# Two heads of the first batch move from the float32 path to the float16 path in a fused attention and feed-forward kernel

## The chip, the cores and the metric

One core of a Trainium2 chip runs the whole program. The metric is the device time in microseconds, the median over several executions. One execution is also profiled: all rows below are from that one, with times from the start of its span.

## What is computed

Eight batches of eight heads, 576 positions of 64 elements; the result of attention is the input x (4608 tokens of 512) of a gated feed forward with 1536 hidden units.

```
scores = (q @ k.T) / 8                       # (8, 8, 576, 576)
cum    = cumsum(max(s, 0))                   # s: (8, 8, 576)
scores = where(causal, -1e9, scores + min(-(cum[:, None] - cum[None, :]), 0))
attn   = exp(scores - max(scores));  attn = attn / (sum(attn) + 1e-9)
x      = (attn @ v) laid out as (8 * 576, 512)
out    = (sigmoid(x @ w_gate) * (x @ w_val)) @ w_out
```

The inputs are float32 or float64 (the weights are decoded from 64-bit words where they come wide), the output is float32.

## The kernel before

The work is written as a loop over ticks `n`, five for each of the 64 heads (`i, t = divmod(n, 5)`), one for each tile of 128 query rows (the first tile has 64). A scheduler of the language then sets the order of each engine's instructions from the order in the program and from priorities: what is written under `first()` goes ahead of the rest. Tiles come from pools with one to ten buffers; a tile that is written again waits for the readers of the old one.

There are two ways through attention.

* The float32 path, for the first `NN` heads (before: `NN = H = 8`, all of batch 0). `n_load` loads a pair's queries and keys; `n_prep` transposes them on TensorE (`nq_ps`, L558) and copies them from PSUM on ScalarE into `nq` and `nk`; `n_s` makes the scores with one float32 matmul for each piece (L575); `n_max` does bias, row maximum (VectorE, L584) and exponential (ScalarE, L587); `n_turn` transposes the weights on TensorE (`nt_ps`, L596) and copies them (L597); `n_av` multiplies with v in float32 (L605); `n_x` transposes x on TensorE (`nx_ps`, L629) and splits it into two float16 parts (L631, L632).
* The float16 path, for all other heads. Every operand is split into a high and a low float16 part. `qk_square`, `qk_scale` and `split_qk` scale and split queries and keys (L357 to L390); one DMA transpose brings them into `T` (L395) and two DMAs swap the halves of the keys (`swap_k`, L400, L401); `split_v` splits v (L430, L431) and copies a part of it by DMA (L436); `s_part` makes the scores with two matmuls for each piece (L446, L447); `bias_row` (L455), `mask_part` (GpSimd, L461) and `max_part` (L471, L474) are bias, mask, maximum and exponential; `p_part` splits the weights (ScalarE L478, VectorE L483 and L491) and transposes them with two DMA transposes into `pt` (L494); `av_part` multiplies with v, 50 small matmuls a head (L506 to L511); `x_part` divides, `split_x` splits x (L527, L528) and transposes it by DMA (L529).

All DMA transposes, loads and swaps of attention are issued from SP's queue, in order; the weights of the feed forward come from ScalarE's queue.

The feed forward works on 18 groups of 256 tokens and 12 slices of 128 hidden units. A unit `(g, f)` is 24 matmuls of 256 columns into `gv` (L657, 48 narrower ones where a group lies in two batches), a tanh (L662), a gate product into `t2` or, in groups 0 and 1, `t2f` (L664), two float16 parts of the hidden slice (`ffn_mid`, L672, L673), and the output matmuls (`ffn_out`, L687). Group 0 needs x of all four pairs of heads of batch 0. From tick `NE` on the first 24 units are given at 1.5 times two units in a tick; with them come the rest of the 18 weight steps (`weight_step`: decode on ScalarE and VectorE, L272 to L275, split, L287 to L293). After them the rate follows the progress of attention, batch by batch; after the last head the remaining units run alone.

In the loop, `NE` stands in three places: where the units begin, as the lower bound of the ticks in which the scores and products of the float16 path have priority, and as the end of the early weight steps.

Of the kernel before, what the change touches and what calls it, by code (L numbers as in the profile page):

```python
# [23 lines left out]
def tile_attention_then_gated_ffn(  # L24
# [12 lines left out]
    B, H, S, D = q.shape  # L37
# [12 lines left out]

    SETS = (((0, 1, 2), (0, 1, 3), 6), ((3, 4), (0, 4), 9))
    PAD = NTL * P - S
    NN = H
    LAG = 3

    ctx.enter_context(nc.allow_low_precision("operands are split into exact high and low parts"))
# [62 lines left out]
    def first(now=True):  # L119
        return tc.high_priority(1000) if now else ExitStack()  # L120
# [287 lines left out]
    def spread_crow(i):  # L408
        spread = nc.gpsimd.partition_broadcast(crow[i], crow[i][0:1] if i > 0 else rel[0:1])  # L409
        if i > NN:  # L410
            tc.keep_in_program_order(spread)

    def load_v(p):
        b, h0 = divmod(2 * p, H)
        t = wp.tile([P, 5, 2, D + 1], F32, tag="v32", name=f"v32_{p}")
        nc.gpsimd.memset(t[64:, 4], 0.0)
        if 2 * p < NN:
            nc.gpsimd.memset(t[:, :, :, D:], 1.0)
# [19 lines left out]
    def s_part(i, t):  # L438
        w = TILES[t][2]
        c0 = S + t * P - PAD  # L440
        lhs = T[i].rearrange("p a n -> p (a n)")[:, c0 : c0 + P]
        pieces = [(0, w)] if w <= 512 else [(0, w // 2), (w // 2, w)]
        S_ps[i, t] = []
        for a, b_ in pieces:
            ps = score_bank(f"s{i}_{t}_{a}")
            nc.tensor.matmul(ps[:, : b_ - a], lhs, T[i][:, 0, a:b_], start=True, stop=False)  # L446
            nc.tensor.matmul(ps[:, : b_ - a], lhs, T[i][:, 2, a:b_], start=False, stop=True)  # L447
            S_ps[i, t].append((ps, a, b_))

    def bias_row(i):  # L450
        if i < NN:
            rl[i] = crow[i]
            return
        r = wp.tile([P, S], F32, tag="rl", name=f"rl{i}")
        nc.vector.tensor_scalar(r, crow[i], qkc[i // 2][1][:, 0:1], None, ALU.mult)  # L455
        rl[i] = r

    def mask_part(i, t):

        q0, m, w = TILES[t]  # L460
        nc.gpsimd.affine_select(rl[i][:, q0:w], rl[i][:, q0:w], pattern=[[-1, m]], compare_op=ALU.is_ge,  # L461
                                fill=-MASKED if i < NN else MASKED, base=0 if i < NN else m - P,
                                channel_multiplier=1)
# [32 lines left out]
    def av_part(i, h_):  # L496
        p, j = divmod(i, 2)
        if i not in AV:
            AV[i] = pp.tile([P, NTL, D + 1], F32, tag="av", name=f"av{i}", bufs=1)
        pt = PT.pop((i, h_))  # L500
        ts, first_block, n = SETS[h_]
        for t, b0 in reversed(list(zip(ts, first_block))):
            for kb in range(t):
                v_ = v16[p][:, kb, j]
                hi, lo = pt[:, b0 + kb], pt[:, LOW[t] + kb]
                nc.tensor.matmul(AV[i][:, t], hi, v_[:, D : 2 * D + 1], start=kb == 0, stop=False)  # L506
                nc.tensor.matmul(AV[i][:, t, 0:D], hi, v_[:, 0:D], start=False, stop=False)  # L507
                nc.tensor.matmul(AV[i][:, t], lo, v_[:, D : 2 * D + 1], start=False, stop=False)  # L508
            v_ = vx[p][:, t, j]
            nc.tensor.matmul(AV[i][:, t], pt[:, b0 + t], v_[:, D : 2 * D + 1], start=t == 0, stop=False)  # L510
            nc.tensor.matmul(AV[i][:, t, 0:D], pt[:, b0 + t], v_[:, 0:D], start=False, stop=True)  # L511

    def x_part(i):
        p, j = divmod(i, 2)
        a = AV.pop(i)
        d = wp.tile([P, 2, NTL], F32, tag="er", name=f"er{i}")
        nc.vector.tensor_scalar(d[:, 0], a[:, :, D], 1e-9 * PSCALE, None, ALU.add)
        nc.vector.reciprocal(d[:, 1], d[:, 0])
        if j == 0:
            xq[p] = wp.tile([P, NTL, P], F32, tag="xq", name=f"xq{p}", bufs=1)  # L520
        nc.vector.tensor_tensor(xq[p][:, :, 64 * j : 64 * j + 64], a[:, :, 0:D],
                                d[:, 1].rearrange("p (t o) -> p t o", o=1).to_broadcast([P, NTL, D]), ALU.mult)

    def split_x(p):
        x16 = wp.tile([P, 2, NTL * P], F16, tag="x16", name=f"x16_{p}", bufs=1)
        src = xq.pop(p).rearrange("p t n -> p (t n)")
        nc.scalar.activation(x16[:, 0], src, AF.Copy)  # L527
        nc.vector.tensor_tensor(x16[:, 1], src, x16[:, 0], ALU.subtract)  # L528
        nc.sync.dma_start_transpose(x_of(*divmod(p, NPAIR)).rearrange("p l (t n) -> p (l t) n", n=P),  # L529
                                    x16.rearrange("p l n -> p (l n)"))  # L530
# [38 lines left out]
    def n_s(i, t):  # L569
        q0, m, w = TILES[t]  # L570
        p, j = divmod(i, 2)
        nS[i, t] = []
        for a, b_ in [(0, w)] if w <= 512 else [(0, w // 2), (w // 2, w)]:
            ps = score_bank(f"s{i}_{t}_{a}")
            nc.tensor.matmul(ps[:, : b_ - a], qT[i][:, q0 : q0 + P], kT[p][:, a:b_], start=True, stop=True)  # L575
            nS[i, t].append((ps, a, b_))
# [143 lines left out]
    load_v(0)  # L720
    n_prep(0)

    NE, NOFF = 44, 87
    FPT = 1.5
    EARLY = 18
    VSQ = 65
# [3 lines left out]
    for n in range(nticks + 12):  # L730
        if n == NTL * EARLY:
            more_room()
        i, t = divmod(n, NTL)
        if i < NN:
            with first():
                n_s(i, NTL - 1 - t)
                if t == 0:
                    bias_row(i)
        elif n < nticks:
            if t == 0:  # L740
                bias_row(i)
            with first(NE <= n < NOFF):
                s_part(i, NTL - 1 - t)
        if 2 <= n < nticks + 2:
            a, z = divmod(n - 2, NTL)
            if a < NN:
                with first():
# [16 lines left out]
                    n_av(a, t_)  # L764

        if t == 1 and NN <= i - 2 < NH:
            with first(NE <= n < NOFF):
                av_part(i - 2, 1)
                av_part(i - 2, 0)
                x_part(i - 2)  # L770
            if i % 2 == 1:
                split_x((i - 2) // 2)
# [165 lines left out]
```

## Time and profile before

| | |
|---|---|
| three runs | 1151.61, 1154.59, 1155.06 us; median 1154.59 us |
| profiled execution | 1150.75 us, span 1149.0 us |
| mean granted TensorE clock | 0.981 |
| TensorE matmul (PE) busy | 1093.9 us, 95% of the span |
| TensorE weight load (PEld) | 856.3 us, 75% |
| VectorE (DVE) | 774.6 us, 67% |
| ScalarE (ACT) | 748.6 us, 65% |
| GpSimd (POOL) | 261.9 us, 23% |
| DMA packets moved | 157.62 MB, mean 137 GB/s |
| largest groups | L657 613.5 us, L687 314.8 us (both PE) |

Shares over the whole span mix stages. The first 260 us hold all of batch 0, the weights and the first groups; most of the rest is feed forward beside attention, and the last 200 us feed forward alone. A matmul's record includes its way through the array, so that records that follow each other overlap; the price of one in a row is the distance of the starts.

### The profile page before, as it was taken

The numbers are of one execution on the slowest core, as the hardware profiler recorded it, in microseconds if no ns is written. First come the engines' busy times: TensorE is split into PE (matmuls) and PEld (weight loads), VectorE is DVE, ScalarE is ACT, GpSimd is POOL, SyncE is SP. The second block draws the span as 40 slices with busy tenths as digits, with TensorE's granted clock in tenths as the row PEclk, the third lists the DMA queues.
The fourth block names the chain that finished last, engine by engine and source line by source line (L and its number), as shares of the span: only waits on it lengthen the run. The fifth ranks groups of instructions, "written<-read, shape, count | busy, mean of one in ns | idle before, by whom it ended". The sixth has DMA issues, their size and how long they took to land.

```text
span 1149.0 us, 30327 instructions
## 1 busy us (share of the span) xinstructions
PE 1093.9 (95%) x11644; PEld 856.3 (75%) x11644; DVE 774.6 (67%) x2393; ACT 748.6 (65%) x1465; POOL 261.9 (23%) x570
## 2 busy tenths in 40 slices
PE   6787889989999999999999999999999999999997
PEld 4566677758777887788777777778877887787775
DVE  6889899866777777775565677777777775222221
ACT  6989778667677777676665677767776765233222
POOL 5625233222132222121211122212222221000000
PEclk9879899999999999999999999999999999999999
DMA  9776778996989888778646488868887764000000
GB/s 266 214 212 164 178 144 183 185 186 135 165 170 174 165 173 169 141 146 145 137 81 136 89 183 164 162 145 181 145 162 144 142 123 88 13 20 19 1 19 19
DMA packets 445102, 157.62 MB, mean 137 GB/s; under 512 B 403551, under 2 KB 435295, under 8 KB 444958
## 3 DMA queue, kind: packets, MB, share of 16 engines
q1 hardware_dynamic: 418398, 127.12, 57.1%
q10 hardware_dynamic: 23040, 16.78, 4.9%
q0 software_dynamic: 3520, 11.80, 3.0%
q8 instruction: 91, 1.49, 0.6%
q14 instruction: 53, 0.43, 0.1%
HBM read 56.92 MB, written 9.58 MB: 58 GB/s over the span
## 4 chain that ended last, share of the span: by engine, by line
PE 51%; issue 25%; DMA 6%; DVE 5%; ACT 3%; POOL 2%; SPq 1%; POOLq 0%; ACTq 0%; DVEq 0%
PE gv L657 28%; PE o L687 14%; PE s L447 2%; PE s L446 2%; DMA v<-in_v_dram 2%; DMA qk<-in_q_dram 1%; POOL rl L461 1%; PE av L506 1%; PE av L508 1%; DVE e L471 1%; PE av L507 1%; DMA pt<-p 1%; SPq L420 1%; ACT e L474 1%; PE av L510 1%
## 5 line engine op out<-in xcount | busy, mean ns | idle before, releaser
L657 PE MATMUL gv<-x,w 128*128 128x256 f16 (+3 forms) x6912 | 613.5, 246 | 5.4 <-DVE t2f L664 2.9
L657 PEld LDWEIGHTS <-w 128*128 128x128 f16 x6912 | 534.0, 98 | 61.7 <-issue 5.3
L687 PE MATMUL o<-w2all,h 128*128 128x512 f16 x1296 | 314.8, 379 | 0.0
L461 POOL TENSOR_SCALAR_AFFINE_SELECT rl<-rl 128x64 f32<-128x64 f32 (+1 forms) x280 | 111.3, 398 | 519.6 <-DVE em L471 464.3
L474 ACT ACTIVATE e<-e,em 128x576 f32<-128x576 f32 x280 | 154.7, 554 | 92.5 <-DVE em L471 90.5
L687 PEld LDWEIGHTS <-h 128*128 128x128 f16 x1296 | 123.7, 98 | 108.0 <-issue 1.7
L662 ACT ACTIVATE th<-gv,scb 128x256 f32<-128x256 f32 (+3 forms) x288 | 111.2, 411 | 138.4 <-PE gv L657 137.6
L664 DVE SCALAR_TENSOR_TENSOR t<-th,gv 128x256 f32<-128x256 f32 x192 | 80.0, 417 | 132.8 <-ACT th L662 131.6
L471 DVE CUSTOM_DVE_ANT_0 e<-s,rl,qkcf 128x288 f32<-128x288 f32 x280 | 135.6, 485 | 29.9 <-PE s L447 24.5
L672 ACT ACTIVATE h<-t,hsc 128x256 f16<-128x256 f32 x192 | 96.6, 503 | 80.1 <-DVE t L664 80.0
L483 DVE SCALAR_TENSOR_TENSOR p<-e,p 128x384 f16<-128x384 f32 x224 | 101.9, 494 | 40.1 <-ACT p L478 39.3
L673 DVE SCALAR_TENSOR_TENSOR h<-t,hsc,h 128x256 f16<-128x256 f32 x192 | 93.1, 485 | 43.4 <-ACT h L672 43.0
L478 ACT ACTIVATE p<-e 128x1152 f16<-128x1152 f32 x112 | 112.1, 1001 | 3.2 <-DMA pt<-p 0.5
L506 PE MATMUL av<-v,pt 128*128 128x65 f16 x560 | 68.0, 193 | 5.3 <-DMA pt<-p 5.3
L446 PE MATMUL s<-T 128*128 128x288 f16 (+2 forms) x246 | 64.8, 281 | 5.2 <-DMA T<-qk 3.8
L695 POOL DMA_DIRECT2D out_dram<-osb x36 | 20.4, 566 | 212.1 <-ACT osb L694 211.2
L507 PE MATMUL av<-v,pt 128*128 128x64 f16 x560 | 68.0, 192 | 0.0
L508 PE MATMUL av<-v,pt 128*128 128x65 f16 x560 | 68.0, 194 | 0.0
L447 PE MATMUL s<-T 128*128 128x288 f16 (+2 forms) x246 | 61.8, 279 | 1.7 <-DMA T<-T 1.6
L506 PEld LDWEIGHTS <-pt 128*128 128x128 f16 x560 | 52.4, 97 | 11.8 <-DMA pt<-p 6.9
L409 POOL PARTITION_BROADCAST cr<-cr x63 | 58.1, 923 | 4.1 <-DMA cr<-cum_d 4.0
L455 DVE TENSOR_SCALAR rl<-cr,qkcf 128x576 f32<-128x576 f32 x56 | 29.1, 519 | 40.0 <-POOL cr L409 39.8
(155 smaller groups left out, 1440.7 us busy)
## 6 DMA issues: line engine op xcount, KB each, us to landing
out_dram<-osb POOLq DMA_DIRECT2D x36, 256.0 KB, 2.9
v<-v SPq DMA_DIRECT2D x56, 162.5 KB
v<-in_v_dram SPq DMA_DIRECT2D x64, 128.0 KB
T<-T SPq DMA_DIRECT2D x82, 72.0 KB
t2f<-in_v_dram SPq DMA_DIRECT2D x20, 288.0 KB
qk<-in_q_dram SPq DMA_DIRECT2D x17, 288.0 KB
qk<-in_k_dram SPq DMA_DIRECT2D x17, 288.0 KB
w2all<-in_moe_w_gate_dram ACTq DMA_DIRECT2D x7, 512.0 KB
```

What stands on the lines that cost most here:

```text
L446: nc.tensor.matmul(ps[:, : b_ - a], lhs, T[i][:, 0, a:b_], start=True, stop=False)
L461: nc.gpsimd.affine_select(rl[i][:, q0:w], rl[i][:, q0:w], pattern=[[-1, m]], compare_op=ALU.is_ge, fill=-MASKED if i < NN else MASKED, bas ...
L471: nc.vector.tensor_tensor_reduce(e_t[t][:, a:b_], ps[:, : b_ - a], rl[i][:, a:b_], c, init, ALU.add, ALU.min, acc)
L474: nc.scalar.activation(e_t[t][:, :w], e_t[t][:, :w], AF.Exp, bias=init, scale=-1.0)
L478: nc.scalar.activation(p_s[h_][:, 0], e_s[h_], AF.Copy, scale=PSCALE)
L483: nc.vector.scalar_tensor_tensor(flat[:, LOW[t] * P : (LOW[t] + t) * P], e_t[t][:, : t * P], PSCALE, flat[:, kb * P : (kb + t) * P], ALU.m ...
L506: nc.tensor.matmul(AV[i][:, t], hi, v_[:, D : 2 * D + 1], start=kb == 0, stop=False)
L657: nc.tensor.matmul(ps[:, gv, a:e], w1[f][:, cc, gv, wl], x_of(b, cc)[:, xl, c0 + a : c0 + e], start=(c == 0), stop=(c == 3 * NC - 1))
L662: nc.scalar.activation(th[:, a:e], ps[:, 0, a:e], AF.Tanh, scale=scb[b][:, f : f + 1])
L672: nc.scalar.activation(h[:, 0], t2, AF.Copy, scale=hsc[:, f : f + 1])
L673: nc.vector.scalar_tensor_tensor(h[:, 1], t2, hsc[:, f : f + 1], h[:, 0], ALU.mult, ALU.subtract)
L687: nc.tensor.matmul(ps[:m], h[:, hl, tt * P : tt * P + m], w2[f][:, wl], start=(f == 0 and c == 0), stop=(f == NF - 1 and c == 2))
```

## The change

`NN` becomes 6: heads 6 and 7, the last pair of batch 0, take the float16 path, so that their queries, keys, weights and x are transposed by DMA and no longer by TensorE. `NE` becomes 47, so that the units of the feed forward are given from tick 47 on instead of 44. The lower bound `NE` goes from the two priorities of the float16 path's scores and products.

```
-    NN = H
+    NN = 6
...
-    NE, NOFF = 44, 87
+    NE, NOFF = 47, 87
...
         elif n < nticks:
             if t == 0:
                 bias_row(i)
-            with first(NE <= n < NOFF):
+            with first(n < NOFF):
                 s_part(i, NTL - 1 - t)
...
         if t == 1 and NN <= i - 2 < NH:
-            with first(NE <= n < NOFF):
+            with first(n < NOFF):
                 av_part(i - 2, 1)
                 av_part(i - 2, 0)
                 x_part(i - 2)
```

What this does to the order of instructions shows at three places. On every engine the order is the same again from head 20 on.

SP's queue, the loads of the fourth pair (heads 6 and 7) before: queries, keys and v, then the next head's row of `cum`.

```order
L540 DMA nqk_3_742<-in_q_dram 96x6x64 x2
L540 DMA nqk_3_742<-in_k_dram 96x6x64 x2
L420 DMA v32_3_747<-in_v_dram 128x4x64 x2
L421 DMA v32_3_747<-in_v_dram 64x2x64
L406 DMA cr6_858<-cum_d_114 1x576
```

The same place now; `T6` and `T7` are the transposed queries and keys of heads 6 and 7.

```order
L347 DMA qk32_3_727<-in_q_dram 96x12x64
L347 DMA qk32_3_727<-in_k_dram 96x12x64
L420 DMA v32_3_776<-in_v_dram 128x4x64 x2
L421 DMA v32_3_776<-in_v_dram 64x2x64
L395 DMA_TRANSPOSE T6_849<-qk16_6_844 128x12x96
L406 DMA cr6_880<-cum_d_114 1x576
L400 DMA T6_849<-T6_849 64x576
L401 DMA T6_849<-T6_849 64x576
L436 DMA v32_3_776<-v16_3_981 64x1300 x2
L395 DMA_TRANSPOSE T7_992<-qk16_7_987 128x12x96
```

The transposes, swaps and copies of the pair stand behind the loads, among the next rows; its `pt` and `x3` transposes follow later in the same queue.

TensorE, where the first unit (`gv0_0`) first reads `x3`, the x of heads 6 and 7, before: behind the first scores of head 9 and the transposes of x3.

```order
L447 MATMUL s9_3_0_1542<-T9_1253 128x448
L629 MATMUL nx_ps_3_3_1296<-ident_88,nx3_1180 128x128 x2
L657 LDWEIGHTS w1_0_66
L657 MATMUL gv0_0_1349<-x3_133,w1_0_66 128x256
L657 LDWEIGHTS w1_0_66
```

The same place now: behind the products of heads 6 and 7 and most of those of head 8 (`av8`).

```order
L510 MATMUL av8_1970<-v32_4_1163,pt1_8_1309 128x65
L511 LDWEIGHTS pt1_8_1309
L511 MATMUL av8_1970<-v32_4_1163,pt1_8_1309 128x64
L657 LDWEIGHTS w1_0_66
L657 MATMUL gv0_0_1454<-x3_133,w1_0_66 128x256
L657 LDWEIGHTS w1_0_66
```

Before, the unit stood ahead of all of head 8's products; now most of them stand ahead of it.

VectorE, ahead of the first unit's gate product (L664), before: it stands at place 285 of the engine's rows, in the middle of head 9's maxima (`em9_3`).

```order
L632 SCALAR_TENSOR_TENSOR x3_133<-nx_ps_3_3_1296,vsc0_327,x3_133 128x256
L367 TENSOR_SCALAR qk1_5_1336<-qk0_5_1334 128x2
L471 ISA e_1_80,em9_3_0_1669<-s9_3_0_1542,rl9_1405,qkcf4_1094 128x448
L471 ISA em9_3_0_1669 128x1
L125 TENSOR_SCALAR xe_w14_1890<-wtot14_1888 128x1
L664 SCALAR_TENSOR_TENSOR t2f_135<-th0_0_1374,gv0_0_1349 128x256
```

The same place now: it is at 332, behind all of head 9's maxima (`em9_0`), the splits of head 10's queries and keys (L390) and a part of head 9's weights (L483, L491).

```order
L390 SCALAR_TENSOR_TENSOR qk16_10_1360<-qk32_5_1287,qksc5_1338,qk16_10_1360 96x6x64
L483 SCALAR_TENSOR_TENSOR p16_1_82<-e_1_80,p16_1_82 128x384
L483 SCALAR_TENSOR_TENSOR p16_1_82<-e_1_80,p16_1_82 128x512
L491 SCALAR_TENSOR_TENSOR p16_1_82<-e_1_80,p16_1_82 128x2x64
L517 TENSOR_SCALAR er8_2011<-av8_1970 128x5
L471 ISA e_0_79,em9_0_0_1762<-s9_0_0_1639,rl9_1344,qkcf4_1108 128x64
L471 ISA em9_0_0_1762 128x1
L664 SCALAR_TENSOR_TENSOR t2f_135<-th0_0_1479,gv0_0_1454 128x256
```

47 more VectorE instructions stand ahead of it.

More of the change, by code (lines that the diff above doesn't have):

```diff
@@ L52, in tile_attention_then_gated_ffn @@
     PAD = NTL * P - S
-    NN = H
+    NN = 6
     LAG = 3
@@ L721, in tile_attention_then_gated_ffn @@
     n_prep(0)
-    NE, NOFF = 44, 87
+    NE, NOFF = 47, 87
     FPT = 1.5
@@ L741, in tile_attention_then_gated_ffn @@
                 bias_row(i)
-            with first(NE <= n < NOFF):
+            with first(n < NOFF):
                 s_part(i, NTL - 1 - t)
@@ L766, in tile_attention_then_gated_ffn @@
         if t == 1 and NN <= i - 2 < NH:
-            with first(NE <= n < NOFF):
+            with first(n < NOFF):
                 av_part(i - 2, 1)
```

## Prediction

> **What bounds the kernel now.** I read the page's slices first, then the busy time by stretch, then TensorE's waits, then the groups by line. In the slices (40 of 28.7 us; tenths busy) TensorE is at 9 from slice 9 on; ahead of that it is not, and there VectorE and ScalarE stand at 7 to 9.
>
> ```profile
> PE   6787889989999999999999999999999999999997
> DVE  6889899866777777775565677777777775222221
> ACT  6989778667677777676665677767776765233222
> ```
>
> The stretches below are cut at VectorE's milestones: the start of head 5's row maxima (80.7), the first unit's gate product in `t2f` (L664, 135.5), unit 11 of group 0 (176.5), unit 11 of group 1 (240.7), unit 1 of group 2 (266.6). Columns: stretch, its length, busy us of PE, PEld, DVE, ACT, POOL, granted clock, DMA share, GB/s.
>
> ```profile
> 80.70:135.50 54.80, 43.29 (x265) 33.52 (x265) 47.54 (x135) 46.06 (x88) 21.70 (x39) 0.84 0.74 187
> 135.50:176.50 41.00, 34.91 (x392) 29.43 (x392) 38.08 (x112) 32.25 (x55) 12.89 (x21) 1.00 0.77 151
> 176.50:240.70 64.20, 60.09 (x618) 46.22 (x619) 54.70 (x193) 50.00 (x99) 19.43 (x41) 1.00 0.91 183
> 240.70:266.60 25.90, 24.32 (x229) 14.97 (x227) 16.80 (x51) 16.37 (x32) 7.29 (x13) 1.00 0.71 167
> 400.00:1149.00 749.00, 741.83 (x8187) 581.07 (x8184) 448.98 (x1418) 441.23 (x874) 125.23 (x298) 1.00 0.57 114
> ```
>
> From 400 us on TensorE is busy 741.8 of 749.0 us (99%), so this part has a fixed length, and the order there is the same before and after. The change is therefore worth what it does to the moment at which the program enters that part. Ahead of it, VectorE is busy 47.5 of 54.8 us (87%) before the first unit and 38.1 of 41.0 (93%) in group 0; TensorE has the higher share only from 176.5 on. TensorE's waits from 100 to 400 us say the same: few, and for transposes and for VectorE.
>
> ```profile
> PE av L506 <- DMA pt<-p: 5.3, 5, 2.0
> PE gv L657 <- DVE t2f L664: 2.9, 3, 1.7
> ```
>
> **TensorE's share of the change.** Heads 6 and 7 lose float32 scores, transposes and products, and get float16 ones. Starts in order of time give the price of one (start, us, engine, line; a float32 matmul has two records):
>
> ```profile
> 103.72 0.97 PE L575 MATMUL s<-nk,nq 128*128 128x448 f32 x2
> 104.53 1.00 PE L605 MATMUL na_ps<-v,p 128*128 128x65 f32 x8
> 105.36 0.76 PE L575 MATMUL s<-nk,nq 128*128 128x320 f32 x2
> 106.86 0.49 PE L596 MATMUL nt_ps<-ident,e 128*128 128x128 f32 x3
> 107.18 0.78 PE L605 MATMUL na_ps<-v,p 128*128 128x65 f32 x6
> 135.60 0.19 PE L506 MATMUL av<-v,pt 128*128 128x65 f16 x1
> 135.63 0.19 PE L507 MATMUL av<-v,pt 128*128 128x64 f16 x1
> 160.93 0.35 PE L446 MATMUL s<-T 128*128 128x448 f16 x1
> 161.12 0.35 PE L447 MATMUL s<-T 128*128 128x448 f16 x1
> ```
>
> A float32 head: 1600 score columns at 0.81 us per 448 are 2.9 us; 15 products at 0.83/4 = 0.21 are 3.1; 15 transposes at 0.32/3 = 0.11 are 1.6; half of a pair's 17 transposes of queries, keys and x, at the same 0.11, 0.9. Together 8.5. A float16 head: 3200 columns at 0.19 per 448 are 1.4, 50 products at 0.03 are 1.5, together 2.9. So TensorE loses 5.6 us a head, 11 in all. By the order all of this lies ahead of the first unit; from the first unit to group 2 TensorE's work is the same within 1 us. There TensorE waits already, so I cost the 11 us at nothing; they would count in full only if TensorE were what delays the first unit.
>
> **VectorE's share.** In the order 287 VectorE instructions stand ahead of the first L664 before, 334 now. The kinds that differ, with their prices (busy us, mean ns of one):
>
> ```profile
> L471 DVE CUSTOM_DVE_ANT_0 e<-s,rl,qkcf 128x288 f32<-128x288 f32 x280 | 135.6, 485 | 29.9 <-PE s L447 24.5 <-POOL rl L461 3.0 <-DVE p L491 0.2
> L471 DVE DVE_READ_ACCUMULATOR2_ANT em<- 128x1 f32 x336 | 27.3, 81 | 0.0
> L584 DVE CUSTOM_DVE_ANT_0 e<-s,cr 128x288 f32<-128x288 f32 (+4 forms) x40 | 16.7, 423 | 6.5 <-PE s L575 3.5 <-POOL cr L461 2.4
> L483 DVE SCALAR_TENSOR_TENSOR p<-e,p 128x384 f16<-128x384 f32 x224 | 101.9, 494 | 40.1 <-ACT p L478 39.3
> L491 DVE SCALAR_TENSOR_TENSOR p<-e,p 128x128 f16<-128x128 f32 x168 | 40.9, 270 | 0.0
> L455 DVE TENSOR_SCALAR rl<-cr,qkcf 128x576 f32<-128x576 f32 x56 | 29.1, 519 | 40.0 <-POOL cr L409 39.8
> L388 DVE SCALAR_TENSOR_TENSOR qk<-qk,qksc,qk 96x384 f16<-96x384 f32 x22 | 13.5, 615 | 1.5 <-ACT qk L387 1.4
> L431 DVE SCALAR_TENSOR_TENSOR v<-v,vsc,v 128x640 f16<-128x640 f32 x28 | 24.7, 882 | 15.0 <-ACT v L430 14.8
> L528 DVE TENSOR_TENSOR x<-xq,x 128x640 f16<-128x640 f32 x28 | 22.9, 820 | 0.8 <-ACT x L527 0.8
> L293 DVE SCALAR_TENSOR_TENSOR w2all<-wa,wscale,w2all 128x1024 f16<-128x1024 f32 x6 | 7.6, 1274 | 0.6 <-ACT w2all L292 0.5
> L367 DVE TENSOR_SCALAR qk<-qk 128x2 f32<-128x2 int32 x28 | 4.7, 168 | 0.7
> L632 DVE SCALAR_TENSOR_TENSOR x<-nx_ps,vsc,x 128x320 f16<-128x320 f32 (+1 forms) x8 | 4.1, 507 | 0.3 <-ACT x L631 0.3
> ```
>
> Row maxima: 15 pieces of L471 more, with their read-outs, at 0.485 + 0.081 = 8.5 us; 12 of L584 fewer, at 0.423 and the same read-out, -6.0. Low parts of the weights p: 10 of L483 (4.9) and 7 of L491 (1.9). Bias rows: 3 of L455 (1.6). Low parts of queries and keys: 3 of L388 and 3 of L390 at 0.615 (3.7). One split of v (0.9), one of x (0.8), one weight split L293 (1.3) that has moved ahead of the unit, 14 small scale instructions at 0.17 (2.4), two L632 fewer (-1.0). The sum is +19.0 us of records. Records of one engine overlap: in these two the next starts 0.37 us after a start whose record lasts 0.44.
>
> ```profile
> 80.71 0.44 DVE L584 CUSTOM_DVE_ANT_0 e<-s,cr 128x288 f32<-128x288 f32 x1
> 81.08 0.07 DVE L584 DVE_READ_ACCUMULATOR2_ANT em<- 128x1 f32 x1
> ```
>
> At 0.07 for each of the 47, 3.3 us go off: +15.7 us of VectorE ahead of the first unit. (Two heads alone are about 10 of it; the rest is head 9's maxima and splits, which the order now puts ahead of the unit too.)
>
> The stretch before the first unit has 54.8 - 47.5 = 7.3 us of idle VectorE. If the new work filled all of it, the unit would be 15.7 - 7.3 = 8 us later; if the idle share stayed at 87%, 15.7/0.87 = 18 us. I take the next stretch's 93%: (47.5 + 15.7)/0.93 = 68.0 us instead of 54.8, +13 us, since there the same mix of float16 heads and weight splits already runs.
>
> **Behind the first unit.** Up to unit 11 of group 0 the orders put equal VectorE work to within three instructions: 0. Up to group 2 VectorE has about 5 us less to do (this is what came earlier), TensorE the same. TensorE is busy 34.9 + 60.1 + 24.3 = 119.3 of 131.1 us there, so between 0 and some 6 us of its idle time could close; I take 2, because its largest wait, for pt, stays. After that the orders are equal and nothing is given back. Sum: +13 - 2 = +11 us.
>
> **ScalarE, DMA and GpSimd** are costed at nothing. ScalarE changes two conversions of p for five copies out of PSUM in each head, nearly even (2.0 against 2.4 us), and adds splits of q, k, v and x against three copies of q and k and one of x, about 1 us a head; VectorE's 87% against ScalarE's 46.1/54.8 = 84% hides it, barely.
>
> ```profile
> L478 ACT ACTIVATE p<-e 128x1152 f16<-128x1152 f32 x112 | 112.1, 1001 | 3.2 <-DMA pt<-p 0.5
> L597 ACT COPY p<-nt_ps 128x384 f32<-128x384 f32 x40 | 18.2, 474 | 3.9 <-PE nt_ps L596 3.5 <-issue 0.3
> ```
>
> SP's queue gets two T transposes, four swaps, two copies of v, four pt transposes and one x transpose. From 80 to 160 us (queue, packets, MB, share):
>
> ```profile
> q1 hardware_dynamic: 22848, 6.75, 42.0%
> q10 hardware_dynamic: 13486, 7.29, 31.9%
> ```
>
> Four float16 heads' T and pt share the 42% (33.6 us), so two heads add at most some 17 us of 80: 74% becomes up to 95%. Cover enough on average, not where w_out's loads on q10 stand.
>
> **Clock.** TensorE's granted clock is 0.84 from 80.7 to 135.5 and 1.00 behind it; with 11 us less work in a longer stretch it has less to do there. The Trainium skill, TensorE: Matmul & The Clock Gate, Part 1, says that an idle window of about 3.4 us halves the clock until a busy one has passed; the rows agree in direction. By that rule the first unit would start cold and lose up to half of 3.4 us, and the sum would be +13 rather than +11.
>
> **Rivals.** (1) Latency: the four float16 heads 6 to 9 have no feed forward beside them, and each waits in turn for T, swap, pt and x through DMA, on SP's one queue. The chain of work shows what each took:
>
> ```profile
> 110.11 5.50 DMA T<-qk
> 172.83 4.45 DMA pt<-p
> 242.40 4.30 DMA x<-x
> ```
>
> VectorE would then stay at 80% or less: (47.5 + 15.7)/0.80 = 79 us, +24 to the first unit, less 2: about +22. Against it: T6 stands right behind v of pair 3 on SP, long ahead of its use. (2) Absorbed: all 7.3 us of idle close (+8) and the 6 us behind it too: +2, no change to be told. For it: more independent streams in a list order. (3) Faster: TensorE, with float32 work at a half clock, is what holds VectorE at 87%; without it VectorE runs full (+8), and all 11.8 us of TensorE's idle time up to group 2 close: 8 - 12 = -4. It decides if the first unit comes less than about 9 us later. Against it: 16 us of VectorE work must fit in 7 us of holes in any case.
>
> **How the numbers follow.** The profiled run took 1150.75 us with a span of 1149.0; +11 makes 1162. The median of the runs is 1154.59, 3.8 above the profiled one, so I predict 1165. Chances: the forecast (+4 to +18) 0.63; latency (+18 to +28) 0.10; absorbed (within 3.5 us either way, which is 0.3% and about what can be told from no change) 0.14; faster (-4 and below) 0.13. Slower 0.73, same 0.14, faster 0.13. The range 1151 to 1175 leaves out the faster case and the upper part of the latency case, about 2 in 10; the likeliest's own is 1158 to 1173.
>
> **What would show it.** The first L664 at 144 to 153 us instead of 135.5, VectorE over 90% busy from 80 us to there, TensorE's busy time there down by about 10 us and its clock not above 0.84; group 2's unit 1 about 11 us late, and a tail from 400 us on that is as long as before. Wrong: a first L664 within 8 us of before, or a long VectorE wait for pt, T or x (then it was latency).

## The result, and the profile after

The changed kernel takes 1167.8 us (median of four runs, 1166.03 to 1170.93) against 1153.1 us for the kernel before (four runs, 1149.59 to 1155.06): a ratio of 1.0119 with a 95% interval of 1.0093 to 1.0146, slower by 14.7 us. The profiled execution took 1170.93 us with a span of 1169.0, the longest of the four; its span is 20.0 us longer than that of the profile before, so times read from the two profiles overstate the loss by some 5 us.

The page's slices of the kernel after (29.2 us each):

```profile
PE   6787488989999999999999999999999999999997
DVE  6888899874778777775666577777777775222221
PEclk9856599999999999999999999999999999999999
```

The clock's slices before (28.7 us each):

```profile
PEclk9879899999999999999999999999999999999999
```

Counted from 0, TensorE's slice 4 falls from 8 to 4 tenths, and its clock is at 5 and 6 tenths in slices 2 to 4, where it was at 7 to 9. VectorE stays at 8 there. From slice 9 on TensorE is as full as it was.

The stretches are cut at the same milestones as in the prediction: head 5's maxima, the first L664, unit 11 of group 0, unit 11 of group 1, unit 1 of group 2; then the last 749 us, and the way from the first L664 to group 2 in one piece. Columns: length, busy us of PE, PEld, DVE, ACT, POOL, granted clock, DMA share, GB/s.

```profile
81.60:155.50 73.90, 46.96 (x305) 34.14 (x305) 64.16 (x175) 53.40 (x89) 26.57 (x43) 0.60 0.82 184
155.50:198.40 42.90, 38.95 (x420) 33.35 (x420) 39.02 (x115) 31.51 (x58) 13.79 (x25) 0.96 0.81 149
198.40:262.10 63.70, 56.52 (x537) 42.62 (x535) 53.76 (x184) 46.82 (x92) 17.19 (x37) 0.95 0.92 176
262.10:290.00 27.90, 27.90 (x256) 17.05 (x255) 12.91 (x37) 14.88 (x30) 5.05 (x11) 1.00 0.51 121
420.00:1169.00 749.00, 742.37 (x8199) 581.72 (x8196) 448.43 (x1418) 440.84 (x873) 124.89 (x298) 1.00 0.57 114
155.50:290.00 134.50, 123.37 (x1208) 93.02 (x1208) 105.68 (x332) 93.21 (x178) 36.03 (x72) 0.96 0.80 156
```

The same last way, before:

```profile
135.50:266.60 131.10, 119.32 (x1237) 90.62 (x1238) 109.57 (x353) 98.62 (x185) 39.61 (x75) 1.00 0.83 170
```

The last 749 us hold the same matmul time as before (742.4 against 741.8 us), so the whole loss arises ahead of them. The stretch before the first unit grew from 54.8 to 73.9 us, and VectorE's work in it from 47.5 to 64.2 us; its share is 87% both times. The DMA share rose from 0.74 to 0.82 of a longer stretch: 54.8 x 0.74 = 40.6 us of all engines' time became 73.9 x 0.82 = 60.6.

VectorE's timeline gives the first gate product and that of unit 1 of group 2:

```profile
155.55 0.41 DVE L664 SCALAR_TENSOR_TENSOR t2f<-th,gv 128x256 f32<-128x256 f32 x1
290.01 0.41 DVE L664 SCALAR_TENSOR_TENSOR t<-th,gv 128x256 f32<-128x256 f32 x1
```

They come 20.0 and 23.4 us later than before (135.5 and 266.6), and by the end the lag is 20.0 again. The lag grows head by head: from the start of head 5's maxima to that of head 8's it goes from 0.9 to 12.2 us (80.7 to 81.6, 119.9 to 132.1).

Before, TensorE's two largest waits from 80 to 136 us were these (line, what it waited for: us, times, longest); beside them it waited 0.3 us for pt.

```profile
PE na_ps L605 <- ACT p L597: 3.3, 4, 1.7
PE s L446 <- DMA T<-qk: 2.3, 1, 2.3
```

After, from 81 to 156 us:

```profile
PE s L446 <- DVE em L471: 8.4, 7, 2.6
PE s L446 <- DMA T<-qk: 4.7, 1, 4.7
PE av L506 <- DMA pt<-p: 4.1, 3, 2.5
...
PE s L447 <- DMA T<-T: 2.1, 2, 1.2
```

and those of SP's queue from 70 to 156 us:

```profile
SPq L420 <- PE na_ps L605: 10.0, 2, 6.2
SPq L395 <- DVE wa L274: 6.4, 1, 6.4
SPq L395 <- DMA t2f<-in_moe_w_out_dram: 5.1, 1, 5.1
```

TensorE waits for VectorE's maxima, and 10.9 us for transfers of the float16 path (T, pt and the swaps), where it waited 2.6 us before. In SP's queue the profile puts 6.4 and 5.1 us of a T transpose's (L395) waits down to a weight's decode and to a load of w_out. No single wait has the size of the loss. The chain of waits in this part passes through three transfers, the longest of them the load of the next pair's queries:

```profile
121.85 5.27 DMA T<-qk
...
133.19 7.01 DMA qk<-in_q_dram
...
142.22 4.44 DMA pt<-p
```

### The profile page after: what moved, and what is told of

Read it like the earlier page. It is cut to its first block, busy times and chain, and to the rows that moved or that the text cites. A ratio compares the mean times of both kernels' runs of the same rounds, so it can differ in the third digit from the quotient of the medians.

```text
span 1169.0 us, 30321 instructions
## 1 busy us (share of the span) xinstructions
PE 1101.5 (94%) x11617; PEld 858.6 (73%) x11617; DVE 785.6 (67%) x2420; ACT 752.8 (64%) x1461; POOL 264.3 (23%) x569
## 4 chain that ended last, share of the span: by engine, by line
PE 58%; issue 20%; DMA 4%; DVE 3%; ACT 2%; POOL 1%; SPq 1%; POOLq 0%; DVEq 0%; ACTq 0%
PE gv L657 32%; PE o L687 16%; PE s L446 3%; PE s L447 3%; PE av L506 1%; PE av L508 1%; PE av L507 1%; DVE e L471 1%; DMA qk<-in_q_dram 1%; DMA v<-in_v_dram 1%; DMA T<-qk 1%; POOL rl L461 1%; DMA pt<-p 1%; PE av L510 1%; PE av L511 1%
## 5 line engine op out<-in xcount | busy, mean ns | idle before, releaser
L657 PE MATMUL gv<-x,w 128*128 128x256 f16 (+3 forms) x6912 | 620.1, 247 | 3.8 <-DVE t2f L664 3.8
L461 POOL TENSOR_SCALAR_AFFINE_SELECT rl<-rl 128x64 f32<-128x64 f32 (+1 forms) x290 | 119.4, 413 | 523.0 <-DVE em L471 463.8
L474 ACT ACTIVATE e<-e,em 128x576 f32<-128x576 f32 x290 | 159.5, 554 | 86.1 <-DVE em L471 84.2
L664 DVE SCALAR_TENSOR_TENSOR t<-th,gv 128x256 f32<-128x256 f32 x192 | 80.1, 417 | 132.3 <-ACT th L662 131.4
L471 DVE CUSTOM_DVE_ANT_0 e<-s,rl,qkcf 128x288 f32<-128x288 f32 x290 | 140.3, 485 | 27.3 <-PE s L447 17.9
L483 DVE SCALAR_TENSOR_TENSOR p<-e,p 128x384 f16<-128x384 f32 x232 | 106.9, 501 | 47.4 <-ACT p L478 46.5
L478 ACT ACTIVATE p<-e 128x1152 f16<-128x1152 f32 x116 | 116.0, 1000 | 5.9 <-DMA pt<-p 2.8
L446 PE MATMUL s<-T 128*128 128x288 f16 (+4 forms) x258 | 69.7, 285 | 15.1 <-DVE em L471 10.2
L506 PE MATMUL av<-v,pt 128*128 128x65 f16 x580 | 72.7, 196 | 10.0 <-DMA pt<-p 9.8
L507 PE MATMUL av<-v,pt 128*128 128x64 f16 x580 | 72.8, 195 | 0.0
L508 PE MATMUL av<-v,pt 128*128 128x65 f16 x580 | 72.6, 197 | 0.0
L447 PE MATMUL s<-T 128*128 128x288 f16 (+4 forms) x258 | 66.4, 284 | 3.0 <-DMA T<-T 3.0
L506 PEld LDWEIGHTS <-pt 128*128 128x128 f16 x580 | 55.4, 99 | 17.3 <-DMA pt<-p 12.1
L507 PEld LDWEIGHTS <-pt 128*128 128x128 f16 x580 | 55.6, 99 | 4.8
```

Of the source, the lines that this page charges most:

```text
L471: nc.vector.tensor_tensor_reduce(e_t[t][:, a:b_], ps[:, : b_ - a], rl[i][:, a:b_], c, init, ALU.add, ALU.min, acc)
L474: nc.scalar.activation(e_t[t][:, :w], e_t[t][:, :w], AF.Exp, bias=init, scale=-1.0)
L478: nc.scalar.activation(p_s[h_][:, 0], e_s[h_], AF.Copy, scale=PSCALE)
L483: nc.vector.scalar_tensor_tensor(flat[:, LOW[t] * P : (LOW[t] + t) * P], e_t[t][:, : t * P], PSCALE, flat[:, kb * P : (kb + t) * P], ALU.m ...
L657: nc.tensor.matmul(ps[:, gv, a:e], w1[f][:, cc, gv, wl], x_of(b, cc)[:, xl, c0 + a : c0 + e], start=(c == 0), stop=(c == 3 * NC - 1))
```

## Experiments

Every run is timed against the kernel before on the same chip; ratios are run to kernel before, with the 95% interval. The expectations set these theories against each other: VectorE's added work (V), the latency of the pair's transfers in turn (L), TensorE's low clock (C), and in the later runs the DMA load, TensorE's own work, and the order that the scheduler makes anew for each program.

The order of instructions tells one thing without a run. With `NN` = 8, `NE` = 47 alone or the changed priorities alone leave the order of before on every engine as it was. With `NN` = 6 that is not so: with `NE` = 44 kept, 266 VectorE instructions stand ahead of the first L664, fewer than the 287 before; with `NE` = 47 it is 334, and every engine has the order of the change, whether the priorities are changed or not. So the later start of the units belongs to the change as much as the path of the two heads does, and no run times `NN` = 6 with `NE` = 44. The nearest is the run on another pair below, which keeps `NE` = 44.

**VectorE's work alone.** The kernel before, with 26 instructions of 576 columns put into VectorE's stream:

```
+        if 30 <= n < 43:
+            for _ in range(2):
+                tc.keep_in_program_order(nc.vector.scalar_tensor_tensor(
+                    load, load, 1.0, load, ALU.mult, ALU.mult))
```

> The kernel before with 26 VectorE instructions of 576 float32 columns more, two in each of the ticks 30 to 42, that stand in program order and touch nothing that is needed (some 0.6 us each, 15.6 us in all). The float32 path, its transposes on TensorE and the place of the units stay. Theory V (VectorE's work ahead of the first units sets when the program enters the part that TensorE bounds): slower by 10 to 16 us, as the change. Theory L (the DMA latency of T, swap, pt and x in heads 6 and 7 sets it): 0 to 5 us slower, since VectorE had 7.3 us of holes there. Theory C (TensorE's clock at a half): under 4 us slower, since TensorE's work is the same.

1166.07 against 1152.72 us, ratio 1.0106 [1.0077, 1.0135]. The stretch before its first unit:

```profile
78.80:144.80 66.00, 49.99 (x316) 38.28 (x316) 62.91 (x164) 49.14 (x90) 27.76 (x40) 0.77 0.69 156
```

VectorE is 95% busy (62.9 of 66.0 us) and the first unit comes 9.3 us late, unit 1 of group 2 13.3 us late (279.9). The 26 instructions are 0.747 us each in the records, 19.4 us in all; 21 of them, 16.2 us, lie ahead of the first unit, about as much as the change's 16.6. VectorE work of this size, with no transfer and no TensorE work changed, is enough to make a loss of this size. The way there is not the change's, though: unit 11 of group 1 is only 1.7 us late (242.4 against 240.7), and the lag is back at unit 1 of group 2, where the next batch is first needed.

**TensorE given more matmuls.** The changed kernel, with 168 matmuls whose results nobody reads:

```
+        if 33 <= n < 47:
+            warm = pp.tile([P, 2, GT], F32, tag="gv", name=f"warm{n}")
+            for c in range(12):
+                nc.tensor.matmul(warm[:, 0], ...)
```

> The changed kernel with 12 matmuls of 256 columns in each of the ticks 33 to 46, on a weight tile, into PSUM tiles that nobody reads: 168 matmuls, 18 us of TensorE work at full clock, into its idle time ahead of the first unit. C: the granted clock there rises from 0.60 to 0.85 or more and the time falls by 3 to 8 us below that of the changed kernel. V and L: the clock rises, the time stays as that of the changed kernel or is up to 6 us longer, where the extra matmuls stand ahead of others in TensorE's queue.

1170.65 us, ratio 1.0150 [1.0103, 1.0198]. Before the first unit, and from there to unit 1 of group 2:

```profile
80.50:155.30 74.80, 52.75 (x466) 41.15 (x466) 67.67 (x186) 55.54 (x92) 29.19 (x43) 0.82 0.88 192
155.30:291.83 136.53, 123.23 (x1263) 93.20 (x1262) 104.26 (x332) 93.40 (x177) 39.92 (x72) 1.00 0.77 156
```

The clock before the first unit rose from 0.60 to 0.82, behind it from 0.96 to 1.00, and neither stretch got shorter. This does not settle the clock, for the added matmuls all ran between 101.5 and 124.4 us. There the clock was 1.00, and head 9's maxima came at 137.9 us instead of 144.8. Then it fell back, to 0.50 ahead of the first unit's matmuls and 0.58 during them:

```profile
101.50:124.70 23.20, 21.92 (x203) 19.00 (x203) 21.93 (x62) 17.78 (x30) 10.64 (x14) 1.00 0.71 142
140.00:150.40 10.40, 3.15 (x45) 2.66 (x46) 9.19 (x32) 8.63 (x14) 3.51 (x7) 0.50 1.07 217
150.40:155.30 4.90, 4.90 (x27) 3.53 (x27) 4.90 (x13) 2.50 (x5) 0.00 (x0) 0.58 0.91 173
```

After the change the same two places had 0.50 and 0.65. The order differs too: 344 VectorE instructions stand ahead of the first L664, not 334, and TensorE waited 6.9 us for pt instead of 4.1. So what a clock kept high up to the first unit would be worth is open.

**VectorE's work taken away.** The four runs here leave out the last instruction of a weight's decode (L275, which sets the lowest three bits of the weights): in all 18 weight steps, or from step 6 on.

```
-        nc.vector.scalar_tensor_tensor(a, r[:, :, 0], 29, a, ALU.logical_shift_right, ALU.bitwise_or)
+        if n < 6:
+            nc.vector.scalar_tensor_tensor(a, r[:, :, 0], 29, a, ALU.logical_shift_right, ALU.bitwise_or)
```

The kernel before, without L275 in any step:

> The kernel before without the last VectorE instruction of each weight decode (L275, the or-ing in of the low word's three bits, 1.22 us each, 18 in all, 14 of them ahead of the first unit): the weights lose their last three bits. V: about 17 us of VectorE work less ahead of the first unit, faster by 8 to 15 us. L: the chain of the float32 heads is not a matter of VectorE's load; faster by 0 to 5 us. C: no change.

1161.6 us, ratio 1.0068 [1.0047, 1.0090]: slower with less work. Its order differs from the start; head 1's maxima begin at 32.8 us instead of 25.2, head 3's at 55.6 instead of 43.5. It says nothing on the place in question, and something on the method: an edit that removes 18 instructions can cost 8 us, with the order as the only other thing that differs.

The changed kernel, without L275 in any step:

> The changed kernel without the same instruction (L275), so that VectorE has about as much to do ahead of the first unit as in the kernel before. V: back to the time of the kernel before, within 4 us. L: the chain through DMA remains, 8 to 15 us slower than the kernel before. C: TensorE idles as before in that stretch, so 8 to 15 us slower than the kernel before as well.

1163.54 us, ratio 1.0084 [1.0057, 1.0110]; it has the same late start (head 3's maxima begin at 53.4 us), so it is no clean test either. Between these two kernels without L275 the change costs only 1.9 us (1163.54 against 1161.60). The next two keep the first six steps as they are. The kernel before, without L275 from step 6 on:

> The kernel before without the or-ing in of the low word (L275) for the weight steps from 6 on alone, so that the order of the first 60 us stays as it was; about 8 of these steps lie ahead of the first unit (10 us of VectorE). V: the first unit 6 to 10 us earlier, the time 5 to 10 us shorter. D: the first unit is held by DMA as before, within 3 us.

1149.95 us, ratio 0.9972 [0.9948, 0.9995]: at most a gain of the size that can just be told from none. VectorE's theory had forecast a first unit 6 to 10 us earlier; it came at 140.5 us, 5 us later than before. (That profiled execution took 1155.21 us, 5 us above its own median, so it does not show that a late first unit costs nothing.)

The changed kernel, without L275 from step 6 on:

> The changed kernel without L275 for the weight steps from 6 on. V: 6 to 10 us shorter than the changed kernel, so 5 to 9 us above the kernel before. D: VectorE's busy share falls below 85% ahead of the first unit, TensorE's waits for T, swap and pt grow, and the time stays within 4 us of the changed kernel, 11 to 15 us above the kernel before.

1166.88 us, ratio 1.0106 [1.0057, 1.0155], where 1.0119 was to be undone; from the kernel before without the same instructions it is 16.9 us. The time is what the DMA theory gave, but not for its reason, a VectorE less than 85% busy. The stretch, and head 10's maxima and the first gate product on VectorE (lines one higher there):

```profile
78.30:151.20 72.90, 47.06 (x311) 34.37 (x311) 63.54 (x188) 59.50 (x99) 24.72 (x44) 0.60 0.88 188
```

```profile
148.78 0.50 DVE L472 CUSTOM_DVE_ANT_0 e<-s,rl,qkcf 128x288 f32<-128x288 f32 x1
...
151.20 0.41 DVE L665 SCALAR_TENSOR_TENSOR t2f<-th,gv 128x256 f32<-128x256 f32 x1
```

Attention is back at the pace of before (head 10 begins at 148.8 us, before at 150.6, after the change at 161.8), but the first unit is still 15.7 us late: in its order 343 VectorE instructions stand ahead of the first L664, though the decode lost some. Other work stands in the place of what was removed, and VectorE is 87% busy again.

**DMA alone.** The kernel before, with eight DMA transposes of ten 128 x 128 blocks into an unused buffer:

```
+        if 30 <= n < 46 and n % 2 == 0:
+            tc.keep_in_program_order(nc.sync.dma_start_transpose(xslots[4]..., w1[0]...))
```

> The kernel before with eight DMA transposes of 128 x 1280 float16 more on SP's queue, one in every second of the ticks 30 to 44, from a weight tile into a slot of x that is not yet in use: 80 blocks of 128 x 128, where the two heads of the change add 84. VectorE's and TensorE's work stay. Theory V (VectorE's load alone): within 4 us of the kernel before. Theory D (DMA and SP's queue are a second bound, close behind VectorE): slower by 6 to 15 us, with the first unit 6 to 12 us later.

1159.23 us, ratio 1.0039 [1.0015, 1.0063]. The stretch, and TensorE's wait for T:

```profile
79.80:140.60 60.80, 45.65 (x275) 35.68 (x274) 44.81 (x126) 46.77 (x89) 18.69 (x36) 0.82 0.83 190
```

```profile
PE s L446 <- DMA T<-qk: 4.0, 1, 4.0
```

With VectorE doing less in the stretch than before (44.8 us), the first unit is 5.1 us late and the total 0.39% longer, about 5 us: less than the theory of a second bound gave (6 to 15), more than VectorE's alone. They added 60.8 x 0.83 - 40.6 = 10 us of DMA time to the stretch; the change added 20. The order differs here too (278 VectorE instructions ahead of the first L664, not 287), and x2 lost more than 5 us with less work to do. So this run speaks for a price of the transfers and does not prove it.

**TensorE's work added instead.** The kernel before with `NN = 10`: heads 8 and 9 take the float32 path too, so VectorE and DMA have less and TensorE has more.

> The other direction: the kernel before with two heads more, 8 and 9, on the float32 path (NN = 10). VectorE has about 10 us less and SP's queue two heads' transposes less, TensorE 11 us more; the order lets the units of groups 0 and 1 run ahead of these heads. V and D: what the change lost is gained again where VectorE or DMA still bounds, 3 to 10 us shorter. If TensorE is already the bound from the first unit on: its 11 us more are paid in full, 8 to 12 us longer.

1166.53 us, ratio 1.0091 [1.0058, 1.0125]. From its first L664 to unit 1 of group 2:

```profile
138.90:283.60 144.70, 128.45 (x1239) 98.75 (x1240) 102.90 (x326) 94.74 (x180) 30.96 (x68) 0.95 0.65 129
```

The theories of VectorE and DMA had forecast a gain of 3 to 10 us, TensorE as the bound a loss of 8 to 12; the kernel is some 11 us slower. But this is not TensorE's work paid for in this stretch. TensorE is busy 9.1 us longer (128.45 against 119.32) at a clock of 0.95; busy time multiplied by the clock, an estimate of the work, is 122 against 119 us. The order is another: the last gate product of group 1 comes 19 us earlier than before (221.4 against 240.7), and the maxima of head 10 come 20 us later (170.8 against 150.6). So a pair more on either path costs about 1% in these programs, and the run does not say what TensorE's work alone costs.

**Another pair.** Heads 4 and 5 take the float16 path instead of 6 and 7 (`NE` = 44 stays), so that the float16 pair is not part of one chain of four such heads ahead of the first unit:

```
+    F16_EARLY = (4, 5)
+    def f32_head(i):
+        return i < NN and i not in F16_EARLY
```

with `f32_head` in place of the tests on `NN`.

> The same exchange of paths in another pair: heads 4 and 5 of batch 0 take the float16 path, heads 6 and 7 stay on the float32 path, the units are given from tick 44 on. VectorE's, TensorE's and DMA's work are those of the changed kernel, and nearly all of it still lies ahead of the first unit (318 VectorE instructions ahead of it, against 287 before and 334 in the changed kernel), but x of the last pair comes again from TensorE and not at the end of the chain T, scores, p, pt, products, x through DMA. Theory V (work ahead of the first unit, on VectorE and DMA): the first unit 9 to 18 us later than before and the time 9 to 15 us longer, as in the changed kernel. Theory L (the length of the float16 chain of the last two heads is what delays the first unit): the first unit within 6 us of before and the time 0 to 6 us longer.

1167.79 against 1154.64 us, ratio 1.0103 [1.0062, 1.0145]. Before the first unit, and from there to unit 1 of group 2:

```profile
78.50:144.70 66.20, 45.83 (x282) 35.05 (x281) 60.85 (x166) 54.28 (x93) 22.40 (x37) 0.65 0.95 209
144.70:288.20 143.50, 127.14 (x1265) 94.64 (x1264) 112.24 (x348) 100.17 (x186) 39.62 (x75) 0.96 0.79 159
```

The loss cannot be told from the change's, although the pair stands elsewhere and `NE` stays at 44; VectorE's theory gave 9 to 15 us, the latency theory 0 to 6. In the order 318 VectorE instructions stand ahead of the first L664. The first unit is only 9.2 us late, unit 1 of group 2 21.6 us: here the work shows up behind the first unit.

**The last transfer taken out of the chain.** The changed kernel, with x of heads 6 and 7 transposed on TensorE (`n_x`) instead of by DMA (`split_x`); x of the first 64 positions of these heads then comes from the wrong half of a tile.

```
+                if i == NN + 3:
+                    with first():
+                        n_x((i - 2) // 2)
+                else:
+                    split_x((i - 2) // 2)
```

> The changed kernel, in which x of heads 6 and 7 alone is transposed by TensorE out of xq, as on the float32 path, and not by DMA (split_x replaced by n_x for this pair). In the order the first unit stands again ahead of head 8's products (316 VectorE instructions ahead of it). L: the first unit 5 to 10 us earlier than in the changed kernel, the time 4 to 9 us shorter. V: VectorE's work as a whole is the same, within 3 us of the changed kernel.

1166.0 us, ratio 1.0092 [1.0060, 1.0124].

```profile
80.60:148.60 68.00, 45.63 (x267) 32.99 (x267) 58.65 (x159) 47.84 (x82) 23.17 (x39) 0.59 0.81 178
148.60:286.10 137.50, 122.94 (x1222) 92.01 (x1220) 110.46 (x349) 98.17 (x184) 36.31 (x75) 0.98 0.85 164
```

The first unit comes 7 us earlier than after the change, and 3 us of that are lost again by unit 1 of group 2 (286.1 against 290.0, with 5 us more VectorE work behind the first unit). That first unit is what the latency theory gave (5 to 10 us earlier), its time (4 to 9 us shorter) is not: the ratio cannot be told from the change's. The same without L275 from step 6 on:

> The same as the last, and without the or-ing in of the low word (L275) for the weight steps from 6 on (the weights lose three bits): VectorE's load and the chain's last step are both relieved. If each of the two holds the first unit as soon as the other is gone: more than both singly, 8 to 14 us shorter than the changed kernel, near the kernel before. V alone: as without the change of x, 1 to 4 us shorter than the changed kernel. L alone: as without the relief of VectorE, 4 to 9 us shorter.

1168.28 us, ratio 1.0110 [1.0081, 1.0140], first unit at 152.8 us: two reliefs together bring nothing either, which no theory gave.

**Both loads together.** The kernel before, with 26 VectorE instructions of 320 columns and sixteen DMA transposes of five blocks each, in the same ticks as above.

> The kernel before with both loads of the change and none of its paths: 26 VectorE instructions of 320 float32 columns (some 0.41 us each, 11 us, where the two heads add about 10) and 16 DMA transposes of five blocks on SP's queue (80 blocks, where the heads add 84), in the ticks 30 to 44; TensorE keeps its float32 work. Theory W (the change costs what its VectorE and DMA work cost in a stretch that is full on both, and TensorE's 11 us less are worth nothing): the two prices add, 9 for VectorE (by x1, scaled) and 5 for DMA (x5), 11 to 17 us slower. Rival (both take the same holes, so that the larger alone counts): 6 to 10 us slower, and the rest of the change's loss would be the float16 chain itself.

1176.74 against 1152.15 us, ratio 1.0212 [1.0185, 1.0239].

```profile
81.05:153.38 72.33, 54.39 (x275) 42.06 (x274) 62.89 (x175) 52.34 (x95) 27.03 (x41) 0.69 0.80 170
```

```profile
SPq L883 <- DMA x<-w: 12.2, 5, 3.8
```

The stretch looks like that of the change (62.9 us of VectorE in 72.3, against 64.2 in 73.9), with TensorE's work left in, and costs 24.6 us instead of 14.7. That is more than either theory gave (11 to 17, and 6 to 10). The two loads do not hide each other. But the added transposes write one buffer in turn, and SP's queue stood 12.2 us for that (L883), which the change has no counterpart of, and the order is again its own; so the 10 us between the two are not the price of TensorE's lost work, nor a sure bound of it.

## Why the prediction was right, and where its steps failed

**Direction and place held; the size is near partly by luck.** Slower, 1167.8 against 1165.0 forecast and inside the likeliest case's own range of 1158 to 1173. The last 749 us kept their length, and the lag is complete by unit 1 of group 2. But the forecast was worked out on the profile, as +11 us, and there the lag is 20.0 us at the first unit, 23.4 at unit 1 of group 2 and 20.0 at the end. The medians differ by less, 14.7 us.

**VectorE's work: right.** Forecast +15.7 us ahead of the first unit, measured 64.2 - 47.5 = +16.6 in the stretch; from the start of the span, as the forecast counted, +15.0 (112.6 to 127.7). x1 shows that such work alone is enough: +9.3 us at the first unit, 1.06% in the total. The forecast took all 47 instructions as the cost of the path; by the order, where the first L664 stands among them is set by `NE` as well.

**VectorE's share: wrong by some 7 us.** The step took 93%, from the next stretch; it stayed at 87%, and 64.2/0.87 is the 73.9 us measured. The first L664 came at 155.5 us, behind the band of 144 to 153, where "the idle share stayed at 87%" had given 18 us. In x1, where VectorE alone got work, its share did rise, to 95%; in the change and in x12, where DMA got work too, it stayed at 87%, and in x9 it was 92%. That the transfers kept the holes open is likely by this, but not shown. The mark "TensorE's busy time there down by 10 us" failed too: it rose by 3.7 us, in a longer stretch at a clock of 0.60 instead of 0.84. Busy time multiplied by the clock, an estimate of the work, goes from 36.4 to 28.2 us, so the work did leave.

**DMA costed at nothing: most likely wrong.** "Two heads add at most some 17 us of 80" was near (20 us more in the stretch); that it would be hidden is what the rows speak against: TensorE's waits for T, pt and the swaps grew from 2.6 to 10.9 us. x5 puts such a load at 0.39%, about 5 us, with the order as a second cause. ScalarE's share fell (46.1 of 54.8 to 53.4 of 73.9 us); nothing here speaks against its zero.

**TensorE's 11 us, costed at nothing: not settled.** x8 adds such an amount and loses about 1%, but in another order; x12 against the change leaves 10 us, in another order too.

**Behind the first unit: -2 was +3.4 in the profile.** VectorE had 3.9 us less to do there, as forecast (about 5), but TensorE was busy 4.1 us longer, and its idle time (11.1 against 11.8 us) did not close. The 4.1 us are not more work: the clock was 0.96 instead of 1.00 there, and busy time multiplied by it is 118 against 119 us. This miss adds to the one ahead of the first unit. By the end of the span the 3.4 us had gone again, where the prediction had that nothing is given back.

**The rivals.** Absorbed and faster are out: 1.0119 [1.0093, 1.0146]. Latency as one chain of four heads is not supported as what makes the loss: x9 breaks the chain up and x10 takes its last transfer out, and the loss stays, though in x10 the first unit did come 7 us earlier. VectorE's largest waits in the stretch are 3.3 us for TensorE's products (L605) and 1.6 for ScalarE, none for pt, T or x. The clock: the rule of the Trainium skill, TensorE: Matmul & The Clock Gate, Part 1, agrees in direction (0.84 to 0.60 with less to do), and its +13 was nearer than +11. Whether that is for its reason is open: x4 raises the mean clock to 0.82 with no gain, but not where the first unit runs.

**What stays open.** How the 14.7 us divide into VectorE, DMA, the later start of the units, the clock and what TensorE gave back. x1 scaled to the change's work ahead of the first unit is 1.06% x 16.6/19.4, or 10 us; up to unit 1 of group 2, where work that had only moved has come back, VectorE had 12.7 us more to do in the change and 19.0 in x1, which gives 8 us. x5 is 9 us if doubled by the DMA time that it added, and 5 us if taken by the blocks that its expectation counts (80 against 84). Less the 14.7 us, the sums leave between nothing and some 5 us for TensorE's relief. That is arithmetic on two runs which each had an order of its own, not a measurement. Taking VectorE work away (x2, x3, x6, x7, x11) could not settle it, since each such program was planned anew and moved by -4 to +8 us. How much the loss hangs on the order shows in what the same change cost without L275: 1.9 us in one pair of programs (x2, x3), 16.9 in the other (x6, x7).

## What to carry to other kernels

Where several engines are each 80 to 90% busy ahead of a part that is bound by one of them, price a moved step on each engine that receives work, DMA as one of them, and do not count on the receiver's holes to close: here its share rose to 95% where it alone got work, and stayed at 87% where DMA got work too. Where a scheduler makes the order, an instruction removed is not relief at its place: other ready work may take it, and a small edit can cost as much as the change under study. Build each part of a change beside the others before calling one of them all of it: `NE` = 47 alters nothing with eight heads on the float32 path, and much with six. Follow more than one milestone: the first unit was 9 us late in two runs whose next milestone was 13 and 22 us late.

## What was not expected of the hardware

Small DMA transposes within the core take long although the DMA share has room: at a mean share of 0.82 a T took 5.3 and a pt 4.4 us from issue to landing in the chain. Eight more of ten blocks, at a share of 0.74 before, went with a loss of about 5 us. And a mean clock of 0.82 instead of 0.60 over 74 us brought no gain in the total, with the clock at 0.50 in the last 10 us ahead of the first unit.
